# Idle products at TensorE's start, ScalarE for block 0's queries, tile 14's last rows and a new order in an attention and routed-MLP kernel

## The chip, the cores and the metric

The kernel runs on one core of a Trainium2 chip. A time is the device time of one execution in microseconds (us), given as the median of several runs. For the kernel before it is 348.62 us (three runs, 348.61 to 348.75). A profile is one execution recorded by the hardware profiler: which instruction ran when on TensorE (PE; its weight loads, PEld, overlap its products), VectorE (DVE), ScalarE (ACT), GpSimd (POOL) and SyncE (SP, which issues most DMAs).

## What is computed

One batch of S = 2048 tokens of D = 448 features goes through an attention layer with 16 query heads and one shared key and value head of 28 features, and then through an MLP that works on eight tokens only. Both are pre-LN with residuals, in bfloat16.

```python
def attention(x, wq, wk, wv, wo):                 # S=2048, D=448, H=16, Dh=28
    q = (x @ wq).reshape(B, S, H, Dh).transpose(0, 2, 1, 3)
    k, v = x @ wk, x @ wv                          # one head for all
    p = softmax(einsum("bhqd,bkd->bhqk", q, k) * Dh ** -0.5)
    o = einsum("bhqk,bkd->bhqd", p, v)
    return o.transpose(0, 2, 1, 3).reshape(B, S, H * Dh) @ wo

def mod_mlp(x, w_r, w_gate, w_up, w_down):         # F=1792, C=8 tokens
    r = x @ w_r
    idx = argsort(-r)[:, :8]
    xs = x[idx]
    y = (silu(xs @ w_gate) * (xs @ w_up)) @ w_down
    return x + scatter_add(zeros, idx, y * sigmoid(r[idx]))

h = x + attention(layernorm(x), ...)
out = h + mod_mlp(layernorm(h), ...)
```

## The kernel before

**Tiles.** The queries are cut into 16 blocks b of 128 rows, the keys into 16 tiles j of 128. One pair (b, j) is a tile of work: four strips of 128 x 512 scores (128 keys; 4 heads x 128 queries each), in PSUM banks. The scores are TensorE's products of K and Q (L823). From scores to P·V there are two ways. In an **A tile** ScalarE takes the exponential of two strips at a time (L888, 128x1024, two per tile), into a ring P, and TensorE sums P·V into one bank called ACC (`pv_op`, L853). In a **D tile** VectorE clips the four strips to int16 (L915, Y, four instructions of 128x512), GpSimd makes two shifted copies of it (L926, Yc), and TensorE sums the three with three constants, which approximates the exponential. The table `_ND` says how many of a block's 16 tiles are D tiles; their sum is 87, so that 169 tiles are A tiles with 338 exponentials. Six of those belong to block 1's first three tiles: they are taken early, at places that `_EARLY` names, into the space that the MLP weights use later (L874, `wg_sb`, `wu_sb`), because bank ACC still holds block 0.

**The head.** x arrives by DMA in six loads: tiles 0, 1, 2 and 3, then fours. `group(g)` takes groups of key tiles ([0], [1], [2,3], [4,5], [6,7], then fours) through layer norm (VectorE: statistics L724 and L726; ScalarE: Ln and Exp for 1/std, L728 and L730; the normalised rows `of` on VectorE, L737 and L746, or for tiles 1 and 2 on ScalarE, L742), TensorE's transposes (L757) that VectorE copies to xnT (L762), and the products for K and V, which VectorE evicts (L772, L785). K is kept twice; for the groups in `_KD` the second copy is a DMA and not a VectorE instruction. `q_project(b)` multiplies xnT of tile b with the spread-out weights (16 products, L628, `wqx`) and evicts them as Q(b): for block 0 in two halves of 128x256, the first by ScalarE (L803) and the second by VectorE (L806), for later blocks as one 128x512 by VectorE.

**After a block.** VectorE copies ACC out (L953), a chain of DMAs and a reciprocal gives the rows' denominators, VectorE scales (L966), TensorE applies wo, VectorE adds x (L996) and takes the statistics of h (L998, L999) and the router's dot product (L1001, `junk` with the sum in column 4 of `st`). `ln2` does the second layer norm in groups of tiles: (0 to 3), (4 to 7), (8 to 11), (12, 13), (14): on ScalarE Ln and Exp for 1/std (L1012, L1014), on VectorE the rows, which are stored to DRAM.

**The tail.** The router works in two stages. When tiles 0 to 13 are done, `stage1` takes each tile's eight best tokens (112 candidates), writes their numbers to `gidx` (L1123), moves them through a DMA to `cidx`, and GpSimd gathers those rows of h (L1127) into the space of `wqx`; the candidates' Ln and Exp follow (`cst`, L1137, L1139). Tiles 14 and 15 are kept on the chip. Block 15's denominators are made without DMAs: VectorE shuffles them (L1156), ScalarE takes Ln and Exp in two halves (L1158, L1160, `Rb`), VectorE scales (L1165). For tile 14, `ln2` scales the router's product by 1/std while it makes it (L1023) and lets ScalarE write the normalised rows (L1026, into xnT's space) and the residual rows (L1030). `last_rows` does the same for tile 15 out of PSUM (statistics L1041, L1042; Ln and Exp L1043, L1045; router value `rp` L1052; rows L1058, L1060). Then come the best eight of 368 values (L1200), the selection of the tokens' rows by one-hot products, the MLP (3 x 56 products), a gather of the eight rows of the output so far (L1256, `base`, after SP has stored tiles 14 and 15), the sum (L1264, `fin`) and the scatter (L1267). Beside that a guard counts whether all denominators lie in a range (L1276, L1278); were it not so, a second, exact program would run, which does not happen here.

**What sets the order.** Every instruction is registered with an engine, a planned duration, what it reads and writes, and a priority. `_Flow.plan()` (L328) is a list scheduler: at each step it chooses by priority among the instructions whose data would be ready within a window (`_WIN`, one per engine), with weights by kind (`_W`), a look-ahead (`_LOOK`) and limits (`_HOLD`, `_LATE`). What it gives is a fixed order per engine and the PSUM bank of each strip; on the chip each engine runs its list strictly in that order and waits by semaphores. So a changed number re-orders rows through the whole program.

## Time and profile before

| | before |
|---|---|
| median of 3 runs | 348.62 us |
| the profiled execution, time | 348.56 us |
| the profiled execution, span of the core | 346.6 us (1.96 us lie around it) |
| mean granted TensorE clock | 0.988 |
| busy: PE, DVE, ACT, POOL | 318.2, 319.4, 325.4, 190.8 us |
| chain of waits: share of ACT, DVE | 83%, 9% |

A row of the timeline reads: start in us, duration, engine, line and operation, output <- input, shape, count, and in brackets the idle time of the engine just before, with what ended it. The table of stretches gives each engine's busy time between two moments. A row of the groups gives total busy time, the mean of one (which overlaps its neighbours, since an engine starts one instruction before the last has drained), and the idle time ahead of them. PEclk is the clock that the profile grants TensorE; in this profile it reads 1.00 from the start up to 330 us.

### The profile page before, as it was taken

Reading aid. Unit: us, or ns where it says so; the run is one execution under the profiler, and the core shown is the slowest. Engines: PE = TensorE matmul, PEld = TensorE weight load, DVE = VectorE, ACT = ScalarE, POOL = GpSimd, SP = SyncE. Lnnn points to the kernel's source line nnn. Section 1 sums busy time; section 2 is a strip of 40 time slices with the busy share of each in tenths; the row PEclk is TensorE's granted clock in tenths of the full one; section 3 lists DMA queues with packets and bytes.
Section 4 is the critical chain, followed back from the end, with each engine's and each line's share of the span. In section 5 each row is a group of like instructions: output and inputs, shape, how many; then the busy total and the mean of one; then the engine's idle time right before and its main releaser. Section 6 shows DMA issues by size and latency. Waiting matters only on the chain.

```text
span 346.6 us, 8725 instructions
## 1 busy us (share of the span) xinstructions
PE 318.2 (92%) x3630; PEld 105.2 (30%) x3630; DVE 319.4 (92%) x662; ACT 325.4 (94%) x387; POOL 190.8 (55%) x206
## 2 busy tenths in 40 slices
PE   3889899999999999999999998999999999999974
PEld 2644232323232322323232322323232322222334
DVE  6998997999988999999899899999999899999874
ACT  5599999999999999999999999999999999999850
POOL 8010475666545648667456566576747456775401
PEclk9999999999999999999999999999999999999995
DMA  6510000000020205020020206020101012152210
GB/s 158 138 40 3 0 3 18 20 17 18 5 85 4 84 4 168 27 60 30 8 80 5 84 4 165 4 46 16 33 4 30 7 58 85 42 152 58 60 36 9
DMA packets 18374, 16.18 MB, mean 47 GB/s; under 512 B 6574, under 2 KB 15438, under 8 KB 18330
## 3 DMA queue, kind: packets, MB, share of 16 engines
q1 hardware_dynamic: 16826, 15.01, 15.5%
q8 instruction: 29, 0.48, 0.6%
...
q0 software_dynamic: 112, 0.12, 0.1%
...
## 4 chain that ended last, share of the span: by engine, by line
ACT 83%; DVE 9%; DMA 3%; PE 3%; issue 0%; POOLq 0%; POOL 0%; ACTq 0%; DVEq 0%
ACT P L888 80%; DVE Y L915 4%; PE ps L628 2%; DMA wqx<-in_A_wq_dram 1%; ACT wg_sb L874 1%; DMA wqx<-n_rows,cidx 1%; DVE bn L724 1%; PE ps L823 1%; DMA cidx<-gidx 1%; ACT wu_sb L874 1%; DVE K L772 0%; ACT wqx L711 0%; DVE Q L806 0%; PE ps L757 0%; DVE gidx L1123 0%
## 5 line engine op out<-in xcount | busy, mean ns | idle before, releaser
L888 ACT ACTIVATE P<-ps 128x1024 bf16<-128x1024 f32 x332 | 306.8, 1287 | 0.0
L926 POOL INT64_ADD Yc<-Y x174 | 178.5, 1037 | 127.7 <-DVE Y L915 112.3
L915 DVE TENSOR_SCALAR Y<-ps 128x512 int16<-128x512 f32 x348 | 220.0, 683 | 12.0 <-PE ps L823 11.3
L823 PE MATMUL ps<-Q,K 32*128 32x512 bf16 (+1 forms) x1024 | 147.1, 386 | 14.1 <-ACT P L888 10.8
L823 PEld LDWEIGHTS ps<-Q,K 32*128 32x128 bf16 (+1 forms) x1024 | 37.7, 91 | 142.9 <-ACT P L888 122.1
L853 PE MATMUL ps<-Yc,Vs 128*32 128x512 bf16 x696 | 63.9, 385 | 0.0
L853 PE MATMUL ps<-P,Vs 128*32 128x512 bf16 x664 | 59.4, 387 | 0.0
L853 PE MATMUL ps<-Y,Vs 128*32 128x512 bf16 x348 | 34.2, 384 | 0.2 <-DVE Ot L953 0.2
L853 PEld LDWEIGHTS ps<-P,Vs 128*32 128x32 bf16 x664 | 14.1, 93 | 28.3 <-issue 26.2
L853 PEld LDWEIGHTS ps<-Yc,Vs 128*32 128x32 bf16 x696 | 15.7, 94 | 21.5 <-issue 15.8
L628 PE MATMUL ps<-xnT,wqx 112*128 112x128 bf16 x256 | 21.6, 229 | 0.0
L628 PE MATMUL ps<-wo_pad,On 128*32 128x448 bf16 (+1 forms) x244 | 18.1, 358 | 1.2 <-DVE Y L915 0.6
L628 PEld LDWEIGHTS ps<-xnT,wqx 112*128 112x128 bf16 x256 | 15.6, 102 | 7.7 <-issue 4.8
L806 DVE TENSOR_SCALAR Q<-ps,qone 128x512 bf16<-128x512 f32 (+1 forms) x16 | 11.6, 727 | 1.0 <-PE ps L628 0.9
L853 PEld LDWEIGHTS ps<-Y,Vs 128*32 128x32 bf16 x348 | 9.1, 94 | 9.3 <-issue 7.4
L966 DVE TENSOR_TENSOR On<-Ot,Rb 128x512 bf16<-128x512 f32 x15 | 11.0, 734 | 0.5 <-DMA Rb<-l_scr 0.5
L757 PE MATMUL ps<-ident,of 128*112 128x128 bf16 x64 | 6.3, 248 | 5.5 <-DVE of L737 5.5
L996 DVE TENSOR_TENSOR of<-ps,x_sb 128x448 bf16<-128x448 f32 x15 | 9.3, 619 | 1.1 <-PE ps L628 1.1
L953 DVE COPY Ot<-ps 128x512 f32<-128x512 f32 x15 | 10.3, 685 | 0.0
L724 DVE BATCH_NORM_STATS2 bn<-x_sb 128x6 f32<-128x448 bf16 x16 | 9.5, 610 | 0.0
L998 DVE BATCH_NORM_STATS2 bn<-of 128x6 f32<-128x448 bf16 x15 | 9.3, 622 | 0.1
L1001 DVE SCALAR_TENSOR_TENSOR junk<-of,w_rb 128x448 bf16<-128x448 bf16 x14 | 8.5, 611 | 0.0
(169 smaller groups left out, 141.4 us busy)
## 6 DMA issues: line engine op xcount, KB each, us to landing
...
```

The source lines that it names most:

```text
L628: return lambda e: e.matmul(o() if callable(o) else o, lhsT=l, rhs=r, start=start, stop=stop)
L724: G.op(DV, lambda e, t=t: e.bn_stats(bn6[:, t, :], x_sb[:, t, :]), 516, reads=[("x", t)], writes=[("bn6", t)], after=[G.last_w[("xnT", 0)] ...
L806: G.op(DV, lambda e, c=c, src=src: e.tensor_scalar(Q[:, b % 3, c[0]:c[1], :], src(), qone[:, 0:1], None, ALU.add), 60 + n * 150, reads=[u. ...
L823: return e.matmul(ps[:, u.b[0] + q, :], lhsT=K[a:a + w, i % 2, j * 128:(j + 1) * 128], rhs=Q[a:a + w, b % 3, :, :].rearrange("p h n -> p ( ...
L853: return e.matmul(ps[32 * i:32 * i + 32, ACC, :], lhsT=Vs[:, v, j, :], rhs=src(i), start=info["first"] == o.idx, stop=info["last"] == o.idx)
L888: G.op(AC, lambda e, u=u, p=p, n=n: e.activation(P[:, p:p + n, :], ps[:, u.b[0]:u.b[0] + n, :], ACT.Exp, bias=EB, scale=OCT), 50.0 + 426.5 ...
L915: G.op(DV, lambda e, u=u, g0=g0: e.tensor_scalar(Y0[:, g0, :].bitcast(I16), ps[:, u.b[0], :], 0.0, TOP - STEP[-1], ALU.max, ALU.min), 599, ...
L926: G.op(PO, lambda e: e.int64_add(Yc[:, c, :, :].rearrange("p a b -> p (a b)").bitcast(I64), Y0[:, 4 * s:4 * s + 4, :].rearrange("p a b -> ...
L953: o = G.op(DV, lambda e: e.tensor_copy(Ot[:, rb, :], ps[:, ACC, :]), 598, reads=[pk(ACC)], writes=[("Ot", rb)], prio=b - 10.0, after=blk[b ...
L966: G.op(DV, lambda e: e.tensor_tensor(On[:, rb, :, :].rearrange("p h n -> p (h n)"), Ot[:, rb, :], Rb[:, rb, :], ALU.mult), 599, reads=[("O ...
L996: G.op(DV, lambda e: e.tensor_tensor(of[:, t, 0:D], hp(), x_sb[:, t, :], ALU.add), 535, reads=[u.key, ("x", t)], writes=[("of", t)], free=u)
L998: G.op(DV, lambda e: e.bn_stats(bn6[:, t, :], of[:, t, 0:D]), 520, reads=[("of", t)], writes=[("bn6", t)])
```

## The change

1. **Idle products at the head.** A new helper `fill` puts 38 products of 128x128 at the head of TensorE's list. They multiply a tile of ones (`idi`) with itself into bank ACC, whose contents the first real product overwrites.
2. **Block 0's queries.** Both halves are evicted by ScalarE.
3. **Planned durations** of the first transposes and of the K and Q products are lowered. They enter the scheduler only.
4. **Tile 14.** Its router product no longer waits for 1/std: it is made like that of all other tiles, right after the statistics, and one new VectorE instruction of one column (`st5`) scales it later. Its Ln waits for the last Exp of block 15's denominators (`late14`), and its two row instructions on ScalarE wait for tile 15's Exp (`late15`), which puts them behind it.
5. **Tail.** `gidx` gets a flag for the scheduler (`lock`), which is used for VectorE instructions that are not to be planned beside a GpSimd instruction; the second guard step waits for the second half of the gated MLP input (`guT`).
6. **Numbers.** `_KD`, `_EARLY`, `_ND`, weights and windows change, so that all rows are re-ordered.

```diff
-_KD = (1, 2, 4)
-_EARLY = (0, 6, 9)
+_KD = (2, 4, 5)
+_EARLY = (0, 0, 6)
-_ND = (2, 7, 6, 3, 7, 7, 6, 5, 5, 7, 6, 5, 4, 5, 6, 6)
+_ND = (2, 6, 6, 4, 6, 7, 6, 5, 6, 7, 4, 5, 8, 4, 6, 5)
...
     G.op(DV, lambda e: e.memset(idi[:, :], 1.0), 100, writes=["idi"])
+    def fill(n, ns, after):
+        G.op(PE, [mm(ps[:, ACC, 0:128], idi[:, :], idi[:, :], True, True) for _ in range(n)], n * ns, reads=["idi"],
+             writes=[pk(ACC)], after=after, prio=-1999)
+
+    fill(38, 107, ())
...
-            if b == 0 and c[0] == 0:
+            if b == 0:
                 G.op(AC, lambda e, c=c, src=src: e.activation(Q[:, 0, c[0]:c[1], :], src(), ACT.Identity, bias=qone[:, 0:1]),
-                     340, reads=[u.key, "qone"], writes=[("Qa", 0)], free=u)
+                     340, reads=[u.key, "qone"], writes=[("Qa" if c[0] == 0 else "Q", 0)], free=u)
...
-        if t != N1:
-            G.op(DV, lambda e: e.scalar_tensor_tensor(junk[:, :], of[:, t, 0:D], 1.0, w_rb[:, :], ALU.mult, ALU.mult,
-                                                      accum_out=st[:, t, 4:5]), 600,
-                 reads=[("of", t), "w_rb"], writes=["junk", ("st4", t)], lock=True)
+        G.op(DV, lambda e: e.scalar_tensor_tensor(junk[:, :], of[:, t, 0:D], 1.0, w_rb[:, :], ALU.mult, ALU.mult,
+                                                  accum_out=st[:, t, 4:5]), 540,
+             reads=[("of", t), "w_rb"], writes=["junk", ("st4", t)], lock=True)
...
             if t == N1:
                 blk14.append(s3)
-                G.op(DV, lambda e, t=t: e.scalar_tensor_tensor(junk[:, :], of[:, t, 0:D], st[:, t, 1:2], w_rb[:, :], ALU.mult,
-                                                               ALU.mult, accum_out=st[:, t, 4:5]), 600,
-                     reads=[("of", t), ("st1", t), "w_rb"], writes=["junk", ("st4", t)], lock=True)
...
+                late14.append(ln)
+                late15.append(G.op(AC, lambda e, t=t: e.activation(xn2[:, 0, :], of[:, t, 0:D], ACT.Identity,
...
+        q = G.op(AC, lambda e: e.activation(st[:, t, 1:2], st[:, t, 0:1], ACT.Exp, scale=-0.5), 200, reads=[("st0", t)],
+                 writes=[("st1", t)])
+        for o in late15:
+            o.deps[q.idx] = False
...
+        for o in late14:
+            o.deps[q.idx] = False
...
-        G.op(DV, lambda e: e.scalar_tensor_tensor(rp[:, N1:N1 + 1], st[:, N1, 3:4], sw[:, 0:1], st[:, N1, 4:5], ALU.mult, ALU.add),
-             62, reads=["sw", ("st3", N1), ("st4", N1)], writes=[("rp", N1)])
+        G.op(DV, lambda e: e.tensor_scalar(st[:, N1, 5:6], st[:, N1, 4:5], st[:, N1, 1:2], None, ALU.mult), 62,
+             reads=[("st1", N1), ("st4", N1)], writes=[("st5", N1)])
+        G.op(DV, lambda e: e.scalar_tensor_tensor(rp[:, N1:N1 + 1], st[:, N1, 3:4], sw[:, 0:1], st[:, N1, 5:6], ALU.mult, ALU.add),
+             120, reads=["sw", ("st3", N1), ("st5", N1)], writes=[("rp", N1)])
...
+            n_ = G.last_w[("guT", 1)][0]
```

The lines of the code after the head stand 6 to 12 lines lower in the changed kernel.

ScalarE's list in the head, before: it starts with tile 1's normalised rows (L742) and block 0's first query half (L803); L728 and L730 are the Ln and Exp of a group's layer norm, L888 and L874 exponentials of A tiles, L874 those of block 1's early tiles.

```order
L742 ACTIVATE of<-x_sb,nb,rstd 128x448 [waits m_dve]
L803 ACTIVATE Q<-ps,qone 128x256 [waits m_pe]
L728 ACTIVATE var<-mv,ebias 128x2 [waits m_dve]
L730 ACTIVATE rstd<-var 128x2 [waits m_act]
L742 ACTIVATE of<-x_sb,nb,rstd 128x448 [waits m_dve]
L888 ACTIVATE P<-ps 128x1024 [waits m_pe] x2
L728 ACTIVATE var<-mv,ebias 128x2 [waits m_dve]
L730 ACTIVATE rstd<-var 128x2 [waits m_act]
L728 ACTIVATE var<-mv,ebias 128x2 [waits m_dve]
L730 ACTIVATE rstd<-var 128x2 [waits m_act]
L874 ACTIVATE wg_sb<-ps 128x1024 [waits m_pe] x2
```

The same place after; there L742 is L748, L803 is L809, L888 is L894, L874 is L880.

```order
L809 ACTIVATE Q<-ps,qone 128x256 [waits m_pe] x2
L734 ACTIVATE var<-mv,ebias 128x2 [waits m_dve]
L748 ACTIVATE of<-x_sb,nb,rstd 128x448 [waits m_dve]
L736 ACTIVATE rstd<-var 128x2 [waits m_act]
L894 ACTIVATE P<-ps 128x1024 [waits m_pe]
L748 ACTIVATE of<-x_sb,nb,rstd 128x448 [waits m_dve]
L894 ACTIVATE P<-ps 128x1024 [waits m_pe]
L880 ACTIVATE wg_sb<-ps 128x1024 [waits m_pe]
L734 ACTIVATE var<-mv,ebias 128x2 [waits m_dve] x2
L736 ACTIVATE rstd<-var 128x2 [waits m_act] x2
L880 ACTIVATE wg_sb<-ps 128x1024 [waits m_pe]
L880 ACTIVATE wu_sb<-ps 128x1024 [waits m_pe] x2
```

Both query halves stand first, tile 1's rows moved behind them, and two pairs of Ln and Exp moved from ahead of the first early exponential to behind it.

VectorE's list in the head, before, up to the eviction of block 1's queries (L806, 128x512), with K (L772), V (L785), xnT (L762) and the statistics (L724, L726) of tiles 1 to 7 ahead of it:

```order
L772 TENSOR_SCALAR K<-ps,kcol 128x128 [waits m_pe]
L785 TENSOR_TENSOR Vs<-ps,vco 128x3x28 [waits m_pe]
L724 BN_STATS bn<-x_sb 128x6 [waits m_dve]
L762 COPY xnT<-ps 112x4x256 [waits m_pe]
L726 BN_AGGR mv<-bn 128x2 [waits m_dve]
L724 BN_STATS bn<-x_sb 128x6
L726 BN_AGGR mv<-bn 128x2
L724 BN_STATS bn<-x_sb 128x6 [waits md7]
L772 TENSOR_SCALAR K<-ps,kcol 128x256 [waits m_pe]
L785 TENSOR_TENSOR Vs<-ps,vco 128x3x2x28 [waits m_pe]
L726 BN_AGGR mv<-bn 128x2 [waits m_dve]
L806 TENSOR_SCALAR Q<-ps,qone 128x512 [waits m_pe]
```

The same place after; block 1's queries are L812, K L778, V L791, xnT L768:

```order
L768 COPY xnT<-ps 112x4x128 [waits m_pe]
L730 BN_STATS bn<-x_sb 128x6 [waits m_dve]
L730 BN_STATS bn<-x_sb 128x6
L778 TENSOR_SCALAR K<-ps,kcol 128x128 [waits m_pe]
L778 TENSOR_SCALAR K<-ps,kcol 128x128
L791 TENSOR_TENSOR Vs<-ps,vco 128x3x28 [waits m_pe]
L812 TENSOR_SCALAR Q<-ps,qone 128x512 [waits m_pe]
L768 COPY xnT<-ps 112x4x256 [waits m_pe]
L732 BN_AGGR mv<-bn 128x2 [waits m_dve] x2
L732 BN_AGGR mv<-bn 128x2
L730 BN_STATS bn<-x_sb 128x6 [waits md7]
L778 TENSOR_SCALAR K<-ps,kcol 128x256 [waits m_pe]
```

Block 1's queries moved ahead of the xnT copy, the K and the V of tiles 2 and 3, and of two statistics; tile 1's second K copy, a DMA before, came in ahead of them.

ScalarE's list at its end, before, from the last Ln of block 15's denominators (L1158) on; L1012 and L1014 are tile 14's Ln and Exp, L1026 and L1030 its rows, L1043 and L1045 tile 15's Ln and Exp:

```order
L1158 ACTIVATE Rb<-Ot 128x256 [waits m_dve]
L1012 ACTIVATE st<-of,ebias 128x1 [waits m_dve]
L1160 ACTIVATE Rb<-Rb 128x256 [waits m_act]
L1014 ACTIVATE st<-st 128x1 [waits m_act]
L1137 ACTIVATE cst<-wqx,ebias 112x1 [waits ms2]
L1139 ACTIVATE cst<-cst 112x1 [waits m_act]
L1026 ACTIVATE xnT<-of,st 128x448 [waits m_dve]
L1030 ACTIVATE of<-of,st 128x448 [waits m_dve,m_act]
L1043 ACTIVATE st<-of,ebias 128x1 [waits m_dve]
L1045 ACTIVATE st<-st 128x1 [waits m_act]
L1058 ACTIVATE xnT<-ps,st 128x448 [waits m_dve]
L1060 ACTIVATE of<-ps,st 128x448 [waits m_dve]
```

The same place after; tile 14's rows are L1031 and L1035, tile 15's Ln and Exp L1048 and L1050:

```order
L1165 ACTIVATE Rb<-Ot 128x256 [waits m_dve]
L1167 ACTIVATE Rb<-Rb 128x256 [waits m_act]
L1019 ACTIVATE st<-of,ebias 128x1 [waits m_dve]
L1144 ACTIVATE cst<-wqx,ebias 112x1 [waits ms2]
L1021 ACTIVATE st<-st 128x1 [waits m_act]
L1146 ACTIVATE cst<-cst 112x1 [waits m_act]
L1048 ACTIVATE st<-of,ebias 128x1 [waits m_dve]
L1050 ACTIVATE st<-st 128x1 [waits m_act]
L1031 ACTIVATE xnT<-of,st 128x448
L1065 ACTIVATE xnT<-ps,st 128x448 [waits m_dve]
L1067 ACTIVATE of<-ps,st 128x448 [waits m_dve]
L1035 ACTIVATE of<-of,st 128x448 [waits m_act]
```

Tile 15's Ln and Exp moved ahead of both of tile 14's rows, tile 14's residual rows became ScalarE's last row instruction, and the candidates' Ln came in ahead of tile 14's Exp.

More of the change, by code (lines that the diff above doesn't have):

```diff
@@ L758, in tr @@
                                              of[:, a + k, ch * CK + cut(a, ch):(ch + 1) * CK + cut(a, ch)], ident[:, :])
-            G.op(PE, [tr(k, ch) for k in range(m) for ch in range(NCH)], m * 4 * (150 if g == 0 else 80),
+            G.op(PE, [tr(k, ch) for k in range(m) for ch in range(NCH)], m * 4 * (100 if g == 0 else 80),
                  reads=[("of", a + k) for k in range(m)] + ["ident"], writes=[u.key], take=u)
@@ L768, in group @@
         G.op(PE, [mm(bank(uk, c=slice(0, w)), wk_rep[0:CK, ch, :], xnT[0:CK, ch, sl], ch == 0, ch == NCH - 1)
-                  for ch in range(NCH)], 4 * (145 if g == 0 else 5 + w / 2.4), reads=[("wkr", r) for r in range(4)] + ["wk_rep"] + [("xnT", t) for t in tl_],
+                  for ch in range(NCH)], 4 * (75 if g == 0 else 5 + w / 2.4), reads=[("wkr", r) for r in range(4)] + ["wk_rep"] + [("xnT", t) for t in tl_],
              writes=[uk.key], take=uk)
@@ L797, in q_project @@
                 G.op(PE, [mm(bank(u, c=slice((h - c[0]) * 128, (h - c[0] + 1) * 128)), wq_pad[0:CK, ch, h, :],
-                             xnT[0:CK, ch, b * 128:(b + 1) * 128], ch == 0, ch == NCH - 1) for ch in range(NCH)], 470 if b == 0 else 430 if b == 1 else 235,
+                             xnT[0:CK, ch, b * 128:(b + 1) * 128], ch == 0, ch == NCH - 1) for ch in range(NCH)], 235,
                      reads=[("wqp", ch) for ch in range(NCH)] + ["wq_pad", ("xnT", b)], writes=[u.key],
@@ L1011, in ln2 @@
         sv = of[:, sl, D:RW].bitcast(F32)
-        G.op(AC, lambda e: e.activation(st[:, sl, 0], sv[:, :, 1], ACT.Ln, bias=ebias[:, 0:1]), 300,
-             reads=[("stf", t) for t in ts] + ["ebias"], writes=[("st0", t) for t in ts])
+        ln = G.op(AC, lambda e: e.activation(st[:, sl, 0], sv[:, :, 1], ACT.Ln, bias=ebias[:, 0:1]), 300,
+                  reads=[("stf", t) for t in ts] + ["ebias"], writes=[("st0", t) for t in ts])
         G.op(AC, lambda e: e.activation(st[:, sl, 1], st[:, sl, 0], ACT.Exp, scale=-0.5), 100, reads=[("st0", t) for t in ts],
@@ L1044, in last_rows @@
              writes=[("st0", t)])
-        G.op(AC, lambda e: e.activation(st[:, t, 1:2], st[:, t, 0:1], ACT.Exp, scale=-0.5), 200, reads=[("st0", t)],
-             writes=[("st1", t)])
+        q = G.op(AC, lambda e: e.activation(st[:, t, 1:2], st[:, t, 0:1], ACT.Exp, scale=-0.5), 200, reads=[("st0", t)],
+                 writes=[("st1", t)])
+        for o in late15:
+            o.deps[q.idx] = False
         G.op(DV, lambda e: e.scalar_tensor_tensor(junk[:, :], hp(), 1.0, w_rb[:, :], ALU.mult, ALU.mult,
@@ L1159, in tail @@
                  writes=[("Rbh", h), ("Rb", rb)])
-            G.op(AC, lambda e, sl=sl: e.activation(Rb[:, rb, sl], Rb[:, rb, sl], ACT.Exp,
+            q = G.op(AC, lambda e, sl=sl: e.activation(Rb[:, rb, sl], Rb[:, rb, sl], ACT.Exp,
                                                        bias=-63.0 * math.log(2.0), scale=-1.0), 330,
-                 reads=[("Rbh", h)], writes=[("Rbh", h)])
+                     reads=[("Rbh", h)], writes=[("Rbh", h)])
+        for o in late14:
+            o.deps[q.idx] = False
         for h in range(2):
```

33 lines of the change are left out of this document (17 added, 16 removed).

## The prediction

> **What bounds the kernel now.** I read first the table of stretches, then the groups, then the timeline of the two ends. The rows of the stretches (start:end, length, then busy us and instructions of PE, PEld, DVE, ACT and POOL, clock, DMA) show where an engine is never idle:
>
> ```profile
> 11.00:40.00 29.00, 26.11 (x278) 13.63 (x276) 26.76 (x67) 26.08 (x36) 2.21 (x3) 1.00 0.13 36
> ...
> 80.00:120.00 40.00, 38.46 (x430) 12.16 (x430) 35.96 (x64) 40.00 (x45) 23.48 (x23) 1.00 0.14 39
> 120.00:160.00 40.00, 38.73 (x421) 11.09 (x420) 39.16 (x75) 40.00 (x47) 25.44 (x25) 1.00 0.21 62
> ```
>
> ScalarE is busy 40.00 of 40 us in the middle; VectorE has between 0.84 and 4.04 us to spare there. What fills ScalarE, and what a D tile costs VectorE, are the groups' two rows (total busy us before the comma):
>
> ```profile
> L888 ACT ACTIVATE P<-ps 128x1024 bf16<-128x1024 f32 x332 | 306.8, 1287 | 0.0
> L915 DVE TENSOR_SCALAR Y<-ps 128x512 int16<-128x512 f32 x348 | 220.0, 683 | 12.0 <-PE ps L823 11.3
> ```
>
> One exponential takes 306.8 / 332 = 0.924 us, one strip of a D tile 220.0 / 348 = 0.632 us. The change keeps 338 exponentials, so a full ScalarE cannot end this middle sooner; time can come only from the head, until ScalarE is full, and from the tail behind the last exponential. ScalarE's head:
>
> ```profile
> 8.26 0.48 ACT L803 ACTIVATE Q<-ps,qone 128x256 bf16<-128x256 f32 x1
> 9.31 0.30 ACT L728 ACTIVATE var<-mv,ebias 128x2 f32<-128x2 f32 x1 [0.57 <-DVE mv L726]
> 9.64 0.20 ACT L730 ACTIVATE rstd<-var 128x2 f32<-128x2 f32 x1
> 10.28 0.76 ACT L742 ACTIVATE of<-x_sb,nb,rstd 128x448 bf16<-128x448 bf16 x1 [0.43 <-DVE nb L733]
> 10.95 2.06 ACT L888 ACTIVATE P<-ps 128x1024 bf16<-128x1024 f32 x2
> 14.52 0.30 ACT L728 ACTIVATE var<-mv,ebias 128x2 f32<-128x2 f32 x1 [1.52 <-DVE mv L726]
> 14.85 0.20 ACT L730 ACTIVATE rstd<-var 128x2 f32<-128x2 f32 x1
> 15.81 0.30 ACT L728 ACTIVATE var<-mv,ebias 128x2 f32<-128x2 f32 x1 [0.75 <-DVE mv L726]
> 16.14 0.20 ACT L730 ACTIVATE rstd<-var 128x2 f32<-128x2 f32 x1
> 16.89 1.02 ACT L874 ACTIVATE wg_sb<-ps 128x1024 bf16<-128x1024 f32 x1 [0.55 <-PE ps L823]
> ```
>
> Between 13.01 and 16.89 ScalarE waits 1.52 + 0.75 + 0.55 = 2.82 us; from 16.89 it never waits until its last exponentials end (317.43 + 9.50 = 326.93):
>
> ```profile
> 317.43 9.50 ACT L888 ACTIVATE P<-ps 128x1024 bf16<-128x1024 f32 x10
> ```
>
> So the span is 16.89 of head, 310.04 of full ScalarE, and 346.6 - 326.93 = 19.67 of tail.
>
> **The head, part by part.** TensorE's rows there:
>
> ```profile
> 5.50 0.65 PE L757 MATMUL ps<-ident,of 128*112 128x128 bf16 x4 [5.50 <-DVE of L737]
> 6.67 0.61 PE L628 MATMUL ps<-xnT,wk_rep 112*128 112x128 bf16 x4 [0.52 <-DVE xnT L762]
> 7.21 1.86 PE L628 MATMUL ps<-xnT,wqx 112*128 112x128 bf16 x16
> ...
> 10.23 0.61 PE L823 MATMUL ps<-Q,K 64*128 64x512 bf16 x2 [0.56 <-DVE nb L733]
> 10.79 0.61 PE L628 MATMUL ps<-xnT,wk_rep 112*128 112x128 bf16 x4
> 11.33 0.61 PE L823 MATMUL ps<-Q,K 64*128 64x512 bf16 x2
> 11.87 0.29 PE L628 MATMUL ps<-wv_sb,xnT 112*128 112x28 bf16 x4
> 12.00 1.08 PE L757 MATMUL ps<-ident,of 128*112 128x128 bf16 x8
> 12.87 1.26 PE L628 MATMUL ps<-xnT,wqx 112*128 112x128 bf16 x12
> ...
> 14.61 1.28 PE L628 MATMUL ps<-xnT,wqx 112*128 112x128 bf16 x20
> ```
>
> The granted clock reads 1.00 all along, but the pace does not: sixteen `wqx` products take 1.86 us at 7.21 and twenty take 1.28 at 14.61. With about 0.2 us for the last to drain this is 0.11 us apart, then 0.057. The twelve at 12.87 lie between, so the pace doubles at about 13.7, some 3.4 us after a stretch without gaps begins at 10.23; the stretch from 6.67 to 9.67 (3.0 us, ended by the 0.56 of idle) had not done it.
>
> *Fill.* The ones that it reads are set at 0.92 to 1.09:
>
> ```profile
> 0.92 0.17 DVE L669 MEMSET idi<- 128x128 bf16 x1 [0.92 <-PEq L1852]
> ```
>
> From about 1.16 its 38 products at 0.107 us last 4.07 us, to about 5.2. TensorE has nothing to do until 5.50, so the fill costs nothing there; were the pace slower, each 0.3 us past 5.5 would move the head by as much. It is 0.6 us longer than the 3.4 that the trace shows were needed, so I take TensorE to run fast from the first transposes on. [...]
>
> *Block 0.* The sixteen products at 7.21 wait for ScalarE's weight copy and don't move; fast, they end at 7.21 + 15 x 0.057 + 0.2, near 8.25 instead of 9.07. ScalarE evicts both halves by 8.25 + 0.48, near 8.75. VectorE did its half late:
>
> ```profile
> 9.70 0.47 DVE L806 TENSOR_SCALAR Q<-ps,qone 128x256 bf16<-128x256 f32 x1
> ...
> 15.69 0.72 DVE L806 TENSOR_SCALAR Q<-ps,qone 128x512 bf16<-128x512 f32 x1
> ```
>
> But ScalarE's new order has the Ln of tiles 2 and 3, tile 1's rows and an Exp ahead of the first exponential. The Ln waits for statistics that VectorE had at about 9.25 (9.31 above), so 9.3 + 0.30 + 0.76 puts the first exponential at about 10.25 instead of 10.95. The second ScalarE half (0.48) is hidden in the wait that stands ahead of 9.31; VectorE saves 0.47.
>
> *Block 1's queries.* What ends the wait at 16.89 is Q(1), which VectorE evicted at 15.69 to 16.41. Tile 1's rows now end at about 10.35, transposes and copy bring xnT to about 11.15, K, V and sixteen fast products to 12.8, and VectorE's row comes at 13.05, since it has moved ahead of xnT, K and V of tiles 2 and 3 (0.69 + 0.53 + 0.33 = 1.55) and of statistics:
>
> ```profile
> 13.12 0.69 DVE L762 COPY xnT<-ps 112x1024 bf16<-112x1024 bf16 x1
> ...
> 14.91 0.53 DVE L772 TENSOR_SCALAR K<-ps,kcol 128x256 bf16<-128x256 f32 x1
> 15.36 0.33 DVE L785 TENSOR_TENSOR Vs<-ps,vco 128x168 bf16<-128x168 f32 x1
> ```
>
> So Q(1) ends near 13.75, its scores near 14.2: 2.7 us earlier than 16.89. Against this stand two pairs of Ln and Exp that lay in waits and now follow full work (between 0.30 + 0.20 = 0.5, if like rows overlap, and twice that; I take 0.7), and new short waits of ScalarE where scores are queued behind transposes of tiles 6, 7, 10 and 11 on TensorE, which need VectorE's rows. The latter the trace doesn't show; the bounds are 0 and 1.0 us (the 0.55 and 0.75 of wait above are the nearest), I take 0.5. Head: 2.7 - 0.7 - 0.5 = 1.5, between 0.4 and 2.1.
>
> **The middle.** All rows are re-ordered, 87 D tiles remain. I take ScalarE to stay full: no gain and, in the likeliest case, no loss.
>
> **The tail.** Its rows on ScalarE, VectorE, SP and GpSimd:
>
> ```profile
> 330.84 0.30 ACT L1137 ACTIVATE cst<-wqx,ebias 112x1 f32<-112x1 f32 x1 [0.86 <-DMA wqx<-n_rows,cidx]
> ...
> 331.28 0.75 ACT L1026 ACTIVATE xnT<-of,st 128x448 bf16<-128x448 bf16 x1
> 332.06 0.76 ACT L1030 ACTIVATE of<-of,st 128x448 bf16<-128x448 bf16 x1
> 332.73 0.28 ACT L1043 ACTIVATE st<-of,ebias 128x1 f32<-128x1 f32 x1
> ```
>
> ```profile
> 331.00 0.63 DVE L1041 BATCH_NORM_STATS2 bn<-ps 128x6 f32<-128x448 f32 x1
> ...
> 333.28 0.28 DVE L1052 TENSOR_SCALAR rp<-st 128x1 bf16<-128x1 f32 x1 [0.67 <-ACT st L1045]
> ```
>
> ```profile
> 332.85 2.70 SPq L640 DMA_DIRECT2D out_dram<-of  x2
> ```
>
> ```profile
> 337.82 0.89 POOL L1256 DMA_INDIRECT base<-out_dram,tok  x1 [9.32 <-DVE tok L1254]
> ```
>
> Tile 15's router value (333.28) waited 0.67 for its Exp, whose Ln stood behind tile 14's rows until 332.73. Its statistics were complete by 331.9. With the rows behind it, Ln and Exp are done near 332.45, and the router value comes when VectorE has summed its own product, near 332.5: 0.75 earlier, at most 0.95. The router product of tile 14 (0.6) moves ahead of block 15's scaling and delays its first half, not its second; `st5` adds one small instruction beside ScalarE's work. The candidates' Ln now stands ahead of tile 14's Exp, and VectorE's statistics of tile 15 behind what follows from both; the guard's second step has moved behind `gidx`, so the gather lands some 0.4 earlier and this mostly fits. Tile 14's residual rows are now written last, so its store is late: it is hidden as long as `base` is gathered after it; the store was issued by 335.55 and the gather at 337.82. The guard's wait for `guT` delays only a flag, off the path. I take 0.7, between 0.1 and 0.95.
>
> **Sum.** 346.6 - 1.5 - 0.7 = 344.4; with the 1.96 around the span 346.36, and with 0.06, by which the median lies above the profiled run, 346.4.
>
> **Rivals.**
>
> 1. *The fill doesn't do what it says*: TensorE stays slow until about 13.7. For: the 3.0 us from 6.67 did not suffice, and the fill is followed by gaps of 0.3 and 0.5 us, which could undo it; against: its length. Then Q(1)'s sixteen products end 1 us later and its scores near 15.3; VectorE's order still gains. Head 0.6: 347.3.
> 2. *VectorE is the bound of the head*: it is busy 26.76 of 29 us from 11 to 40, and the new order gives it tile 1's second K copy (0.4). Head 0.4 to 0.5, about 347.4. Against: it loses 0.47 for Q(0).
> 3. *The gather lands as late as now* (330.84 less the wait's end): the statistics of tile 15 slip by 0.5, tail 0.2: 346.9.
> 4. *Slower: a D tile comes late.* Block 12 now has eight D tiles of 16. If VectorE falls behind there, PSUM banks stay occupied, scores wait and so does ScalarE; a late D tile costs up to 4 x 0.632 = 2.5 us. One such takes the gains away (348.9), two give 351.4; it decides from the second on. For: VectorE had only 0.84 us to spare in 120 to 160. Against: before, blocks 3 to 5 (3, 7 and 7 D tiles, as many as blocks 11 to 13 have now with 5, 8 and 4) lay in stretches with ScalarE at 40.00.
>
> **Chances.** My forecast 0.44; the first rival 0.24, the second 0.10, the third 0.06, the fourth 0.16 (of which 0.03 ends within 0.2%). 0.2%, about what a measurement of this kernel can tell from no change, is 0.70 us: no change is 347.92 to 349.32. The first two rivals reach into it at their upper ends (0.07 together). Faster: 0.44 + 0.24 + 0.10 + 0.06 - 0.07 = 0.77; same 0.07 + 0.03 = 0.10; slower 0.13. The range: the best head and tail give 346.6 - 2.1 - 0.95 + 2.02 = 345.6, and 345.1 if the new waits turn out a gain; above it takes in the first three rivals at their worst (head 0.2, tail 0.1: 348.3) and 0.4 of a partly late D tile, 348.7. The fourth is mostly left out.
>
> **What would show it.** Right: the transposes at 5.5 as a row of four about 0.4 us long instead of 0.65; sixteen `wqx` products in about 1.05; the first exponential near 10.25, the first early one near 14.2; ScalarE at 40.00 of 40 in the stretches from 40 to 320; tile 15's router value 5.6 us behind the last exponential instead of 6.35. Wrong: a wait of ScalarE on scores in block 12's stretch (about 250 to 285), slow products up to 13, or a wait of `fin` on the gather of `base`.

## The result: 15.4 us slower, most of it at the head

| | before | after |
|---|---|---|
| median (4 runs each) | 348.62 us (348.24 to 348.75) | 364.06 us (363.16 to 365.34) |
| ratio, with its 95% interval | | 1.0448 [1.0415, 1.0481] |
| the profiled execution, and its span | 348.56 us, 346.6 us | 365.34 us, 362.6 us |
| first early exponential of block 1 begins | 16.89 | 30.26 |
| last exponential ends | 326.93 | 342.51 |
| tail behind it | 19.67 | 20.09 |

The forecast was 346.4 us (345.1 to 348.7). The prediction cut the span into head, full ScalarE and tail; cut so, after is 13.37 us longer in the head, 312.25 - 310.04 = 2.21 in the middle and 0.42 in the tail: together the 16.0 by which the spans differ. (The small rest of the difference in time, 0.78, lies outside the spans.) The two rows of after that the cut rests on, of ScalarE:

```profile
30.26 1.02 ACT L880 ACTIVATE wg_sb<-ps 128x1024 bf16<-128x1024 f32 x1 [3.22 <-PE ps L829]
...
330.44 12.07 ACT L894 ACTIVATE P<-ps 128x1024 bf16<-128x1024 f32 x13
```

TensorE's rows of after at the head (start, duration, what it does, count, and in brackets the idle time ahead with what ended it):

```profile
1.14 3.66 PE L628 MATMUL ps<-idi 128*128 128x128 bf16 x38 [1.14 <-DVE idi L669]
16.32 0.67 PE L763 MATMUL ps<-ident,of 128*112 128x128 bf16 x4 [11.51 <-POOL ident L678]
17.51 0.61 PE L628 MATMUL ps<-xnT,wk_rep 112*128 112x128 bf16 x4 [0.52 <-DVE xnT L768]
17.91 0.31 PE L628 MATMUL ps<-wv_sb,xnT 112*128 112x28 bf16 x4
21.27 1.86 PE L628 MATMUL ps<-xnT,wqx 112*128 112x128 bf16 x16 [3.04 <-POOL wqx L720]
```

The fill runs where it was expected, but the first transposes, at 5.50 before, begin at 16.32: they wait 11.51 us for `ident`, the identity matrix, which GpSimd makes. Block 0's queries then wait another 3.04 us for a weight copy of GpSimd's. GpSimd's own rows say where that time is:

```profile
0.82 0.10 POOL L666 MEMSET one<- 128x2 f32 x1 [0.29 <-POOLq L1864]
0.85 0.10 POOL L668 MEMSET ebias<- 128x1 f32 x1
9.16 0.28 POOL L676 TENSOR_SCALAR_AFFINE_SELECT tri<-idi 128x128 bf16<-128x128 bf16 x1 [8.21 <-issue]
15.83 0.18 POOL L667 INT64_ADD one<-one  x1 [6.38 <-issue]
15.98 0.28 POOL L678 TENSOR_SCALAR_AFFINE_SELECT ident<-idi 128x128 bf16<-128x128 bf16 x1
16.23 1.69 POOL L703 MEMSET K<- 128x1920 bf16 x1
17.87 1.37 POOL L704 MEMSET Vs<- 128x1536 bf16 x1
...
20.06 1.06 POOL L720 COPY wqx<-wqx 112x448 bf16<-112x448 bf16 x2
```

The two long gaps (8.21 and 6.38) end in "issue": by the profile GpSimd waits for nobody. The same place of before has no such gap:

```profile
0.82 0.10 POOL L666 MEMSET one<- 128x2 f32 x1 [0.29 <-POOLq L1852]
1.07 0.18 POOL L667 INT64_ADD one<-one  x1
...
1.25 0.28 POOL L670 TENSOR_SCALAR_AFFINE_SELECT tri<-idi 128x128 bf16<-128x128 bf16 x1
1.50 0.28 POOL L672 TENSOR_SCALAR_AFFINE_SELECT ident<-idi 128x128 bf16<-128x128 bf16 x1
```

What differs is one place in GpSimd's list. In the built program some rows read only "ISA" with no tensor. They are named PseudoReloadLibraryIndex and carry a number. By the name I read it as that of a code library which GpSimd is to hold for what follows, and call the time that such a row takes a load. No row of the profile shows a load, and the count of DMA packets is the same (18374 in both); that the gaps are loads is a reading, which rests on these rows and on run 4 below. Before, there is one such row (library 1), ahead of the `int64_add`, and the two selects behind it have none of their own:

```
L666 MEMSET one 128x2
L667 ISA
L667 ISA one<-one 128x2
L668 MEMSET ebias 128x1
L670 AFFINE_SELECT tri<-idi 128x128
L672 AFFINE_SELECT ident<-idi 128x128
```

After, the scheduler has put `tri` first. Ahead of it stands a row with library 0, and ahead of the `int64_add` behind it one with library 1, two loads in all; the gaps of 8.21 and 6.38 us are at these two places:

```
L666 MEMSET one 128x2
L668 MEMSET ebias 128x1
L676 ISA
L676 AFFINE_SELECT tri<-idi 128x128
L667 ISA
L667 ISA one<-one 128x2
L678 AFFINE_SELECT ident<-idi 128x128
```

It is GpSimd's planning window, `_WIN` 615.1 to 7.8, that does this: with that number alone set back, the built list has before's order at the head and the lists of the other engines are unchanged; and before with 7.8 alone gets after's order there (both built, not timed).

Away from the head after is nearer to the forecast. The middle is 2.21 us longer, where the prediction had 0.7 + 0.5 = 1.2 for what comes behind the first early exponential; the tail is 0.42 longer, where it had 0.7 shorter. ScalarE's busy time and the granted clock (sixth column and the one after GpSimd's) are full nearly everywhere from 40 on; the largest loss there is near 164:

```profile
120.00:160.00 40.00, 37.83 (x429) 11.26 (x421) 38.76 (x76) 40.00 (x47) 24.66 (x24) 1.00 0.21 61
160.00:200.00 40.00, 38.76 (x437) 10.90 (x441) 36.08 (x64) 39.22 (x43) 24.66 (x24) 0.96 0.15 40
...
240.00:280.00 40.00, 37.88 (x444) 10.88 (x444) 38.02 (x70) 40.00 (x46) 24.66 (x24) 1.00 0.08 22
```

### The profile page after: what moved, and what is told of

Its sections match the earlier page's. It is cut to its first block, busy times and chain, and to the rows that moved or that the text cites. A ratio compares the mean times of both kernels' runs of the same rounds, so it can differ in the third digit from the quotient of the medians.

```text
span 362.6 us, 8811 instructions
## 1 busy us (share of the span) xinstructions
PE 322.0 (89%) x3668; PEld 108.1 (30%) x3668; DVE 319.0 (88%) x662; ACT 325.2 (90%) x388; POOL 191.7 (53%) x206
## 2 busy tenths in 40 slices
DMA packets 18374, 16.24 MB, mean 45 GB/s; under 512 B 6510, under 2 KB 15438, under 8 KB 18330
## 4 chain that ended last, share of the span: by engine, by line
ACT 81%; PE 8%; issue 4%; DVE 4%; POOL 2%; POOLq 0%; DVEq 0%
ACT P L894 79%; PE ps L628 4%; PE ps L829 2%; PE ps L859 2%; DVE Y L921 1%; PE ps L763 1%; ACT wg_sb L880 1%; POOL K L703 0%; POOL Vs L704 0%; POOL wqx L720 0%; DVE Ot L1163 0%; ACT xnT L1065 0%; ACT st L1019 0%; POOL out_dram L1278 0%; ACT of L1035 0%
## 5 line engine op out<-in xcount | busy, mean ns | idle before, releaser
L894 ACT ACTIVATE P<-ps 128x1024 bf16<-128x1024 f32 x332 | 306.5, 1248 | 1.4 <-PE ps L829 1.3
L921 DVE TENSOR_SCALAR Y<-ps 128x512 int16<-128x512 f32 x348 | 218.3, 680 | 11.9 <-PE ps L829 11.1
L829 PE MATMUL ps<-Q,K 32*128 32x512 bf16 (+1 forms) x1024 | 145.6, 388 | 15.1 <-ACT P L894 12.7
L829 PEld LDWEIGHTS ps<-Q,K 32*128 32x128 bf16 (+1 forms) x1024 | 36.7, 91 | 143.3 <-ACT P L894 124.2
L859 PE MATMUL ps<-Yc,Vs 128*32 128x512 bf16 x696 | 64.7, 384 | 0.1
L859 PE MATMUL ps<-P,Vs 128*32 128x512 bf16 x664 | 61.9, 394 | 0.9 <-ACT P L894 0.6
L812 DVE TENSOR_SCALAR Q<-ps,qone 128x512 bf16<-128x512 f32 x15 | 11.2, 743 | 1.1 <-PE ps L628 1.1
L768 DVE COPY xnT<-ps 112x1024 bf16<-112x1024 bf16 (+1 forms) x9 | 5.5, 625 | 4.4 <-PE ps L763 4.3
L730 DVE BATCH_NORM_STATS2 bn<-x_sb 128x6 f32<-128x448 bf16 x16 | 9.3, 607 | 0.0
L763 PEld LDWEIGHTS ps<-ident,of 128*112 128x112 bf16 x64 | 5.0, 150 | 14.4 <-POOL ident L678 11.7
```

The costliest lines, as they stand in the source:

```text
L730: G.op(DV, lambda e, t=t: e.bn_stats(bn6[:, t, :], x_sb[:, t, :]), 516, reads=[("x", t)], writes=[("bn6", t)], after=[G.last_w[("xnT", 0)] ...
L763: return lambda e: e.transpose(psb[0:CK, u.b[0], (ch * m + k) * 128:(ch * m + k + 1) * 128], of[:, a + k, ch * CK + cut(a, ch):(ch + 1) * ...
L812: G.op(DV, lambda e, c=c, src=src: e.tensor_scalar(Q[:, b % 3, c[0]:c[1], :], src(), qone[:, 0:1], None, ALU.add), 60 + n * 150, reads=[u. ...
L829: return e.matmul(ps[:, u.b[0] + q, :], lhsT=K[a:a + w, i % 2, j * 128:(j + 1) * 128], rhs=Q[a:a + w, b % 3, :, :].rearrange("p h n -> p ( ...
L859: return e.matmul(ps[32 * i:32 * i + 32, ACC, :], lhsT=Vs[:, v, j, :], rhs=src(i), start=info["first"] == o.idx, stop=info["last"] == o.idx)
L894: G.op(AC, lambda e, u=u, p=p, n=n: e.activation(P[:, p:p + n, :], ps[:, u.b[0]:u.b[0] + n, :], ACT.Exp, bias=EB, scale=OCT), 50.0 + 426.5 ...
```

## The experiments

Theory: the two library loads, caused by the order on GpSimd, are the loss; without them the change gives about what was forecast. Rivals: the fill harms the head or the clock; the new order costs the middle. Times stand against the kernel before on the same chip.

### 1. The addition first again (c_add_first)

```diff
-    G.op(PO, lambda e: e.int64_add(one64[:, :], one64[:, :], 0), 190, ...)
+    lib = G.op(PO, lambda e: e.int64_add(one64[:, :], one64[:, :], 0), 190, ...)
...
-    G.op(PO, lambda e: e.affine_select(tri[:, :], ...
+    G.head = lib, G.op(PO, lambda e: e.affine_select(tri[:, :], ...
...
+        lib, tri = self.head; [(l.remove(lib), l.insert(l.index(tri), lib)) for l in (orders[PO], seq)]
```

The last line stands at the end of `plan`. All other rows, on all engines, stay as in after.

> The changed kernel with one row of GpSimd's list put back: its first 64-bit add (L667) ahead of its first affine select (L676), every other list as in the changed kernel. Theory A (GpSimd's code): the two rows need code from two libraries; in the new order GpSimd loads one for the select (8.21 us of issue time before 9.16) and another for the add (6.38 before 15.83), in the old order the resident one serves both. Then GpSimd's identity is ready near 2, block 1's early exponentials start near 14 to 15 instead of 30.26, and the time is 347 to 349.5. Theory B (the fill disturbs GpSimd or its instruction supply) and theory C (the re-ordered lists of the other engines): GpSimd still waits, 363 to 365.

Measured: 349.69 us (345.7 to 350.96) against 348.44, ratio 1.0006 [0.9975, 1.0037]. One row put ahead of another takes back all of the loss (the time is 0.19 above the range that theory A gave, and the first early exponential, at 15.69, came later than 14 to 15). But the forecast's gain of 2 us is not there, and the runs spread over 5 us, where those of before lie within 1.3 (they are so uneven that the ratio isn't that of the medians). What spreads is taken up in runs 5 to 12.

### 2. The select first in the kernel before (b_select_first)

```diff
+        lib, tri = self.head; [(l.remove(lib), l.insert(l.index(tri) + 1, lib)) for l in (orders[PO], seq)]
```

> The kernel before with only the opposite edit: the affine select for tri ahead of the first 64-bit add on GpSimd, no fill, all other lists as before. Theory A: the same two waits appear; block 0's query products move from 7.21 to about 21 and the time to 361 to 363.5. Theories B and C: 348.6.

Measured: 360.89 us (360.49 to 361.2) against 348.44, ratio 1.0356 [1.0334, 1.0378]: 12.4 us for one moved row, in a kernel that has nothing else of the change. Its GpSimd rows are after's:

```profile
9.46 0.28 POOL L670 TENSOR_SCALAR_AFFINE_SELECT tri<-idi 128x128 bf16<-128x128 bf16 x1 [8.51 <-issue]
15.64 0.18 POOL L667 INT64_ADD one<-one  x1 [5.90 <-issue]
15.79 0.28 POOL L672 TENSOR_SCALAR_AFFINE_SELECT ident<-idi 128x128 bf16<-128x128 bf16 x1
```

The time is 0.11 below the expected range. Runs 1 and 2 together show that the order of these two rows is the cause of the loss, in either kernel.

### 3. After with one idle product (c_fill_1)

```diff
-    fill(38, 107, ())
+    fill(1, 38 * 107, ())
```

The planned duration is the same, so no row moves.

> The changed kernel with one idle product instead of 38, all lists else the same. Theory A: GpSimd's two waits remain, 363.5 to 365. Theory B: they go, 347 to 350. Theory C: 363.5 to 365 as well.

Measured: 363.11 us (361.53 to 365.46), ratio 1.0436 [1.0381, 1.0492]; the gaps are 8.82 and 5.92. The time is a little below the expected 363.5 to 365; the fill is not the cause of the loss.

### 4. A late use of the other library in the kernel before (b_other_code_late)

```diff
+    lib0 = sb("lib0", [128, 1], F32)
...
+        G.op(PO, lambda e: e.tensor_tensor(lib0[:, :], ebias[:, :], ebias[:, :], ALU.add), 200, ...)
```

One column, used by nobody, behind the candidates' gather in the tail, where a line at the end of `plan` (not shown) puts it. In the built list a row with library 0 stands ahead of it.

> The kernel before with one more GpSimd instruction that computes nothing used: a one-column tensor_tensor, which the build puts in the other library, in GpSimd's idle 9.3 us behind the gather of the candidates. It leaves the other library resident when the program ends. Theory A with residency (the load named in GpSimd's list before the first add costs nothing because the execution before left it there): now the first add waits some 6 to 8 us, the head is 5 to 7 us later, 353.5 to 356.5. If instead the first load of a program is free as such: 348.6, or up to 350 if the late load holds up the last gather.

Measured: 355.38 us (354.99 to 355.48) against 348.44, ratio 1.0193 [1.0172, 1.0213]. Its GpSimd rows:

```profile
7.81 0.18 POOL L667 INT64_ADD one<-one  x1 [6.92 <-issue]
...
343.02 0.18 POOL L1131 TENSOR_TENSOR lib<-ebias 128x1 f32<-128x1 f32 x1 [7.25 <-issue]
```

The load in the tail, 7.25 us, is hidden: the last exponential ends at 321.83 + 12.20 = 334.03 and the span at 353.7, so the tail is 19.67 as before. What costs is the head, where the gap ahead of the `int64_add`, 0.15 in before, is now 6.92, though nothing but an instruction in the tail is new. I read this as a library that stays from one execution to the next: by it before pays nothing only because it ends with the library that it starts with.

### 5 and 6. The fill alone, and the change without it (b_fill, c_add_first_fill_1)

Run 5 is before with the helper and `fill(38, 107, ())`, all other rows as in before. Run 6 is run 1 with run 3's edit.

> The kernel before with the 38 idle products at TensorE's head and nothing else; every list else as before. If a fast TensorE in the head is worth what the prediction said, block 0's query products take 1.05 us instead of 1.86 and the time is 347.6 to 348.2. If the doubled pace falls back in TensorE's gaps, as in the run with the add first (granted clock 0.50 from about 9 to 16 us), block 1's query products are slow again: 348.3 to 349.5, and runs differ by more than those of the kernel before do.

Measured: 348.24 us (347.61 to 348.75) against 348.2, ratio 0.9997 [0.9988, 1.0007]. This lies between the two ranges, no gain can be told, and the runs differ by 1.1 us, no more than those of before (1.3). In the profiled execution the fill did not raise the pace:

```profile
1.14 4.23 PE L628 MATMUL ps<-idi 128*128 128x128 bf16 x38 [1.14 <-DVE idi L669]
5.50 0.64 PE L763 MATMUL ps<-ident,of 128*112 128x128 bf16 x4
6.66 0.61 PE L628 MATMUL ps<-xnT,wk_rep 112*128 112x128 bf16 x4 [0.52 <-DVE xnT L768]
7.06 1.91 PE L628 MATMUL ps<-xnT,wqx 112*128 112x128 bf16 x16
```

> The changed kernel with the add first on GpSimd and one idle product instead of 38. If the fill gains: 350 to 350.5, slower than with 38 (349.69). If the fill only moves the slow stretch: 348.5 to 349.7, with less spread than 345.7 to 350.96.

Measured: 348.36 us (347.39 to 349.13) against 348.2, ratio 1.0003 [0.9993, 1.0013]. This is just below both ranges; with the fill the same list took 349.69, so the fill gains nothing. Here the granted clock reads 1.00 throughout up to 320, but at the head that isn't the pace: sixteen `wqx` products take 1.87 us at 12.41, as in before's slow stretch. With no dip of the clock in the middle the terms can be read one by one. The first early exponential stands at 16.26, so the new order without the fill gives the head 0.63. The middle takes 311.06 (the last exponentials end at 315.00 + 12.32 = 327.32), 1.02 more than before, of which 0.54 is one wait for scores. The tail is 345.8 - 327.32 = 18.48.

### 7 and 8. The code with the old numbers (b_all_code, b_tail_code)

Run 7 is after's code with before's tables and windows; run 8 is that with only the code of the tail changed (no fill, block 0's queries and the planned durations as before). In both the scheduler plans all rows anew.

> All code edits of the change with the old numbers (so the lists are planned with the old weights, windows and tiles per block, and the add comes first on GpSimd). If what is left beside GpSimd's loads is lost by the new order (ScalarE waits 1.6 us on scores in the middle, two pairs of layer norm rows behind the early exponentials), this is 347 to 348.4. If it is lost by the code edits: 349.2 to 350.2.

Measured: 352.34 us (350.76 to 353.36) against 348.2, ratio 1.0108 [1.0084, 1.0131].

> Only the tail's code edits with the old numbers (no fill, block 0's queries as before). By the prediction the tail gains 0.7: 347.7. By the run with the add first, where the tail behind the last exponential was 19.61 against 19.67: 348.3 to 348.5.

Measured: 353.61 us (351.83 to 354.75), ratio 1.0139 [1.0118, 1.016]. Both missed what was expected, in the middle of the program (315.67 us in run 8 and 314.16 in run 7, against 310.04). ScalarE in run 8 (run 7 has waits of 2.13 at 227 and 0.94 at 247, also behind P·V):

```profile
227.55 1.98 ACT L894 ACTIVATE P<-ps 128x1024 bf16<-128x1024 f32 x2 [2.35 <-PE ps L859]
230.03 1.02 ACT L894 ACTIVATE P<-ps 128x1024 bf16<-128x1024 f32 x1 [0.49 <-PE ps L829]
231.54 1.02 ACT L894 ACTIVATE P<-ps 128x1024 bf16<-128x1024 f32 x1 [0.49 <-PE ps L829]
233.06 19.56 ACT L894 ACTIVATE P<-ps 128x1024 bf16<-128x1024 f32 x21 [0.50 <-PE ps L829]
```

The wait of 2.35 comes from VectorE, which in this plan has the statistics and the router product of h ahead of the copy of ACC:

```profile
225.01 0.62 DVE L1006 BATCH_NORM_STATS2 bn<-of 128x6 f32<-128x448 bf16 x1
225.54 0.61 DVE L1008 SCALAR_TENSOR_TENSOR junk<-of,w_rb 128x448 bf16<-128x448 bf16 x1
...
226.17 0.66 DVE L959 COPY Ot<-ps 128x512 f32<-128x512 f32 x1
```

P·V on TensorE waits for that copy, the scores stand behind P·V, and ScalarE behind the scores. The stretches show what follows (TensorE's busy time second, the clock after GpSimd's):

```profile
226.00:228.00 2.00, 1.11 (x11) 0.24 (x11) 2.00 (x7) 0.45 (x1) 0.00 (x0) 0.66 0.00 0
228.00:230.00 2.00, 2.00 (x18) 0.33 (x19) 1.24 (x3) 1.54 (x2) 1.88 (x2) 0.50 0.06 8
...
234.00:236.00 2.00, 2.00 (x29) 0.55 (x29) 1.73 (x4) 1.92 (x4) 0.42 (x1) 1.00 0.00 0
```

The granted clock falls to 0.50, TensorE is then busy all the time, and three more waits follow. So in this re-planned list these two runs price neither the code nor the numbers by itself. That the fallen clock, and not the order, makes the three later waits is read from this one trace and wasn't tried.

### 9 and 10. Runs 1 and 6 again, on one chip (c_add_first_2, c_add_first_fill_1_2)

The same two kernels as in runs 1 and 6.

> The changed kernel with the add first on GpSimd once more, beside the next two on one chip. If the 38 idle products raise TensorE's pace too early, so that it falls back in the gaps behind them (granted clock 0.50 from about 9 to 16 us) at a place that differs from run to run: 348.5 to 350 with a spread of 3 us or more. If its spread was that chip's: 348.0 to 348.8.

> The same with one idle product, once more: 348.0 to 348.7 with a spread under 2 us, granted clock 1.00 in every stretch up to 320.

Measured: with the fill 349.01 us (346.79 to 351.96), ratio 1.0018 [0.9993, 1.0042]; without it 349.32 (348.16 to 350.12), ratio 1.0014 [1.0001, 1.0027], both against 348.69. In the new order the fill makes the time uneven and not better; in the old order (run 5) it did neither. In the profiled execution of run 1 it had raised the pace, and the head lost it again:

```profile
7.49 1.07 PE L628 MATMUL ps<-xnT,wqx 112*128 112x128 bf16 x16 [0.50 <-ACT wqx L717]
9.13 1.04 PE L829 MATMUL ps<-Q,K 64*128 64x512 bf16 x4 [0.57 <-ACT Q L809]
...
11.84 1.87 PE L628 MATMUL ps<-xnT,wqx 112*128 112x128 bf16 x16
```

Sixteen `wqx` products took 1.07 us at 7.49 and 1.87 at 11.84. The stretches between, in which TensorE was idle for 1.01 and 0.57 of 2 us, end in a fall of the granted clock:

```profile
6.00:8.00 2.00, 0.99 (x17) 0.90 (x18) 1.51 (x5) 1.32 (x4) 1.75 (x5) 1.00 0.73 231
8.00:10.00 2.00, 1.43 (x15) 0.52 (x11) 2.00 (x8) 1.85 (x5) 1.02 (x1) 0.76 0.90 248
10.00:12.00 2.00, 1.48 (x16) 1.19 (x15) 1.80 (x7) 2.00 (x5) 0.00 (x0) 0.50 0.68 206
```

In run 9 the same list kept its pace through the head, with more idle time in it:

```profile
8.00:10.00 2.00, 0.73 (x7) 0.12 (x4) 2.00 (x8) 1.36 (x4) 0.58 (x1) 1.00 0.75 222
10.00:12.00 2.00, 1.21 (x20) 1.07 (x21) 2.00 (x7) 2.00 (x5) 0.00 (x0) 1.00 0.69 201
```

The sixteen products of block 1 take 1.05 there, at 11.56, and the early exponential stands at 14.16 instead of run 1's 15.69. So how busy TensorE was in a stretch of 2 us doesn't by itself decide whether the pace falls. Run 10 missed in time (348.0 to 348.7 expected) and in the clock of the middle: the stretch from 120 to 160 had 39.15 of ScalarE and a clock of 0.96.

### 11 and 12. The gaps of the head filled too (c_add_first_bridges, b_fill_bridges)

If gaps of half a microsecond undo the fill, then idle products in them should keep it. Run 11 is run 1 with eight more in each of four gaps (ahead of block 0's K products, its queries, its first scores, and tile 1's K products); run 12 is before with the fill and eight in each of two gaps (ahead of block 0's K products and of its first scores). The line of run 11 that adds them; a line at the end of `plan` (not shown) moves them to their places:

```diff
-    fill(38, 107, ())
+    fill(38, 107, ()); [fill(8, 0, ()) for _ in range(4)]; G.bridge = G.ops[-4:]
```

> The changed kernel with the add first, the 38 idle products, and eight more in each of four gaps of TensorE's head (ahead of block 0's K, block 0's queries, their scores, and tile 1's K), all else as before. If the pace falls because of those gaps: the clock stays 1.00 in the head, block 1's sixteen query products take about 1.05 us instead of 1.87, the first early exponential starts at 14.2 to 14.8 instead of 15.69, and the time is 346.8 to 347.8. If it falls for another reason: as with the 38 alone, 348.5 to 350.

Measured: 346.68 us (346.09 to 347.43) against 348.69, ratio 0.9947 [0.993, 0.9964]. It beats before by 2.0 us, and the runs lie within 1.4 us. TensorE and ScalarE in its head:

```profile
5.54 0.64 PE L763 MATMUL ps<-ident,of 128*112 128x128 bf16 x4 [0.17 <-DVE of L743]
5.98 0.71 PE L628 MATMUL ps<-idi 128*128 128x128 bf16 x8
6.71 0.40 PE L628 MATMUL ps<-xnT,wk_rep 112*128 112x128 bf16 x4
...
11.56 1.05 PE L628 MATMUL ps<-xnT,wqx 112*128 112x128 bf16 x16
```

```profile
10.21 1.00 ACT L894 ACTIVATE P<-ps 128x1024 bf16<-128x1024 f32 x1
...
14.15 1.02 ACT L880 ACTIVATE wg_sb<-ps 128x1024 bf16<-128x1024 f32 x1 [1.38 <-PE ps L829]
...
312.34 12.32 ACT L894 ACTIVATE P<-ps 128x1024 bf16<-128x1024 f32 x13
```

The transposes are still slow (0.64), the K products behind the first bridge fast (0.40). But run 9's profile has the same 0.64 to 0.65 and 0.40 with no bridge between, and the same head (14.16 against 14.15). So the bridges don't make the head faster than the fill can; as the spread of the times suggests, they make that head come in every run. One profile of each can't show this. The last exponential ends at 324.66, 2.27 earlier than before.

> The kernel before with the 38 idle products and eight more in each of the two gaps of TensorE's head (ahead of block 0's K and ahead of its first scores); every other list as before. If the 2.0 us of the run with bridges come from a steady clock in the head alone: 346.5 to 347.2 where before is 348.4 to 348.7. If they need the new order too, in which block 1's queries stand earlier in VectorE's list (here they stay behind tiles 2 and 3, 15.69 before): 0.2 to 0.7 faster than before, first early exponential at 16.2 to 16.7.

Measured: 347.64 us (347.04 to 348.32) against 348.64, ratio 0.9972 [0.9959, 0.9984]. So fill and bridges gain 1.0 us in the old order, between the two expectations. In the profile the early exponential stands at 16.18 instead of 16.89, held by VectorE's Q(1): 0.71 of the gain is the head's. The rest lies in the middle and the tail (309.75 and 19.07 against 310.04 and 19.67), which read about the same in run 5, where the pace at the head was slow.

## Why the prediction was wrong, point by point

**The step that failed** is the part-by-part working of the head. It took the first transposes to stand at 5.50 as before, looked at how rows moved on TensorE, VectorE and ScalarE, and took GpSimd's head as unmoved. In after the transposes stand at 16.32, behind two gaps of 8.21 and 6.38 us on GpSimd. No term and no rival was about GpSimd there, though `_WIN` for GpSimd went from 615.1 to 7.8 and the transposes read `ident`. Run 2 shows that the moved row alone costs 12.4 us, and run 1 that putting it back leaves a ratio of 1.0006: neither the loss nor the forecast's gain. In after and in runs 2 and 3 the second of the two loads took 5.90 to 6.38 us and the first 8.21 to 8.82; the one at the start of run 4 took 6.92. The two built lists would have given a rival of one load more, but not its price: before's own load costs nothing that its trace shows (the add at 1.07), and that in after both count only the runs show.

**Fill** (forecast: fast from the first transposes on). The transposes took 0.64 or 0.65 in runs 5, 9 and 11, and 0.44 and 0.40 in runs 1 and 12. Just behind them the pace was up in runs 9 and 11 too (K products 0.40), in run 5 not (0.61). So 38 products of 3.7 to 4.2 us are too little to count on: the 3.4 that the prediction read from before's trace was one case, and the 4.23 of run 5 did not do it. The first rival's doubt, that gaps of 0.3 and 0.5 us undo the pace, agrees with run 1's trace, where it falls behind gaps of 0.50 and 0.57, and not with run 9's, where it holds behind 0.57 and 0.98. Why the same fill raises the pace in one execution and not in the next was not shown. The spread of 5 us with the fill in the new order, and of 1.4 with bridges, could come from this; the spread of 1.1 in run 5 doesn't need it.

**Block 0, block 1's queries** (first exponential at 10.25, early one at 14.2). Right once the loads are gone and the pace holds: 10.21 and 14.15 in run 11. Without the pace, which is the first rival, the scores were to be ready near 15.3, and the head of 0.6 had the pairs and new waits already taken off. In run 6 the early exponential stands at 16.26; of the 0.63 gained the middle gave back 1.02, and the time was 348.36 and not 347.3. The pace stayed slow longer than the rival had it: four K products at 16.58 still take 1.00 us. (By their own terms the forecast's head is 0.7 to 2.2 and the rival's 0.4, where the prediction writes 0.4 to 2.1 and 0.6.) The second rival, VectorE as the bound of the head, holds in run 12's old order and not in run 11.

**The two moved pairs of Ln and Exp, and new waits** (0.7 and 0.5). The full stretch is 310.51 in run 11, with no wait in it, 0.47 over before's profile; before's list takes 309.75 in runs 2, 4, 5 and 12, so the pairs cost 0.5 to 0.8, as forecast. New waits are none in run 11, 0.54 in run 6, and 1.33 in after (0.54 at 35, 0.30 and 0.49 near 164).

**The middle** (ScalarE full). Right in run 11:

```profile
240.00:280.00 40.00, 38.13 (x440) 11.11 (x438) 39.47 (x74) 40.00 (x46) 25.77 (x26) 1.00 0.05 16
280.00:320.00 40.00, 38.67 (x430) 10.14 (x427) 39.35 (x83) 40.00 (x47) 25.54 (x26) 1.00 0.34 94
```

Wrong in the profiles of runs 1, 9 and 10. In the stretch from 120 to 160 of runs 1 and 10 the mean clock was 0.96 (in run 1 it fell to 0.50, for about 3.4 us) and ScalarE lost 0.69 and 0.85; in the one from 280 to 320 of runs 1 and 9 it lost 0.73 and 0.62 with the clock at 1.00, so a fallen clock isn't the only cause. In after, where everything behind the head comes 13 to 16 us later than in before, the fourth rival's loss did not come either: ScalarE has 40.00 and 39.92 of 40 from 240 to 320.

**The tail** (0.7, between 0.1 and 0.95). This term is mis-sized, and the reason is that it was worked out from one execution. Tile 15's router value comes 6.35 us behind the last exponential in before's profile, but 5.88, 6.00, 5.94 and 5.77 in runs 2, 4, 5 and 12, whose tail list is before's (run 4 has one GpSimd instruction more). With the new tail it comes after 6.15 in after, 6.14 and 6.13 in runs 1 and 9, 5.95 in run 11 and 5.52 in run 6 (forecast 5.6). The whole tail takes 19.07 to 19.67 with the old list and 18.48 to 20.09 with the new one. So no gain of the tail is shown; 18.48 is run 6 alone. In run 11 the tail is 344.7 - 324.66 = 20.04. The granted clock falls 9.2 us behind the last exponential there, and 11.1 behind it in before; but by the mean clocks of the spans (0.987 and 0.988 over 345.0 and 345.5 us) it falls after about 10 in run 12 with a tail of 19.07, and after about 12 in run 9 with 19.99, so this doesn't explain the lengths. What does stays open, within about 1 us. The third rival, a late gather, did not come: the candidates' Ln begins 3.25 behind the last exponential in run 11, without a wait, and 3.91 in before; but it begins at 3.27 in runs 5 and 12 too, with the old list. Nor did `fin` wait for `base`, which starts 4.2 us ahead of it.

**What was forecast, then, was nearly run 11 and not after:** 346.68 against 346.4, but with 32 idle products that the prediction did not have, by a head of 2.74 less 0.47 instead of 1.5, and a tail of -0.37 instead of 0.7. Two misses of opposite sign make the number close: that is luck in part.
